# A gated scan and two MLPs on one core: the second layer runs three pairs of blocks behind, its second products are turned, and the first blocks, two buffers and the last stores change

## The chip, the core and the metric

One core of a Trainium2 chip runs the whole kernel. The metric is the device time of one execution in microseconds (us); the profile also has the span from the first to the last instruction. TensorE (PE) multiplies, VectorE (DVE) and ScalarE (ACT) do the elementwise work, SyncE (SP) issues nearly all DMAs. GpSimd (POOL) does nothing here.

## What is computed

```python
# x, f_logit [2, 6080, 256], all float32; 12160 tokens in all
f = lower_bound + (1 - lower_bound) * sigmoid(f_logit)
h[t] = f[t] * h[t-1] + (1 - f[t]) * x[t]            # a scan along each of the 2 sequences
y1 = relu(h @ w_in1) ** 2 @ w_out1                   # layer 1: 256 -> 2048 -> 256
out = elu(y1 @ w_in2) @ w_out2                       # layer 2: 256 -> 2048 -> 256
```

## The kernel before

**Blocks and slots.** The tokens are cut into 24 blocks: one of 384 (`FIRST`), then 23 of 512. A block passes through layer 1 (`m == 0`) and later through layer 2 (`m == 1`). In each layer its 2048 hidden units are taken in 8 groups of 256 (`KG`), and one group of one block in one layer is a *slot*. Two neighbouring blocks form a pair, and their 16 slots are woven into a *run*. The runs of layer 1 and layer 2 alternate, and layer 2 stands `BEHIND = 2` pairs behind: pair 0 and pair 1 in layer 1, then pair 0 in layer 2, pair 2 in layer 1, pair 1 in layer 2 and so on; at the end two runs of layer 2 stand alone.

**A slot.** Float32 accuracy comes from splitting each factor into a high and a low part (fp32r), so each product is three matmuls. The *first product* (from 256 to 256 hidden units, into the PSUM tile `pc`) uses a scheme with 7 instead of 8 block products: 21 matmuls of 256 columns, 9 of them "first" and 12 "later", with a copy of `pc` (`snap`, L654, ACT) between. In the first four blocks of layer 1 (`PLAIN`) it is 12 matmuls of 512 columns instead (L640). Then come the sums on DVE (L657 to L669), the activation (layer 1: relu and square on ACT; layer 2: two ACT passes and one DVE pass, L688), and the split into `g`: `high_part` on ACT (L693) and `low_part` on DVE (L698). The *second product* (`out_mm`, L725, into the PSUM tiles `acc`) reads `g` some two slots later on PE (`LAG`, `AGE`).

**Second products of the two layers.** In layer 1 the weight is the stationary operand and `g` streams past it, 512 columns at a time: 12 matmuls for a slot, and the result stands with the features in the partitions. In layer 2 it is the other way round: 128 tokens of `g` are stationary and 256 columns of `w_out2` stream past, 24 matmuls for a slot of 512 tokens, and the result stands with the tokens in the partitions. So ACT copies it out (L805) and SP stores rows of 256 numbers (L809).

**Scan.** `add_scan` loads half a block of `f_logit` and `x` (L549, four DMAs each, 32 partitions by 8 pieces of 64 numbers), takes tanh on ACT (L553), turns 32x32 squares on DVE (L558), forms gate and feed (L564, L572) and scans (L585), and keeps the carry (L591). `add_parts` makes the sums (L492 to L500) and the split of a block's input (L508 on ACT or as a cast on DVE, L516 on DVE). A block's scans are kept back until the run before its own: half h of the pair's blocks starts at the earliest when the slot `SPREAD` slots ahead begins.

**Weights.** They come in as pieces (`st`, L320 to L328), are rebuilt (L383 to L392) and split (L409 to L415). The second weight stays in SBUF (`wo0`, `wo1`), the first is written back to DRAM (`keep`, `keep_whole`) and streamed from there once for each run (`ws`, L474/L476).

**Order.** All steps are listed with an engine, a cost, a due time and what they read and write (`Order`). `run` then plays a list schedule with these costs: at each point it takes, of the steps that can start within `HOLD` us on an engine, the one with the earliest due time. That fixes the order of each engine's queue; on the chip every queue runs strictly in this order, and an instruction that has to wait holds up everything behind it.

Of the kernel before, what the change touches and what calls it, by code (L numbers as in the profile page):

```python
# [22 lines left out]
BEHIND = 2  # L23
# [23 lines left out]
class Order:  # L47
# [9 lines left out]
    HOLD = 0.2  # L57
# [104 lines left out]
def kernel(  # L162
# [203 lines left out]
    def add_weights(i, m, kind, c, due, wk=None):  # L366
        t = {}

        def load(e):
            t["st"] = new("st", [P, 2, CE // 2, 2], I32)  # L370
            load_w(nc.scalar if i == 0 else nc.sync, t["st"], m, kind, c)
            if i == 0:
                for k in range(KD):
# [24 lines left out]
        def parts():  # L398
            if kind == 0:
                return t["a"], ws_t[m, c][:, 0, 0:4], ws_t[m, c][:, 1, 0:4]  # L400
            v = t["a"].rearrange("p (k e) i -> p k (e i)", k=2)
            return v, *(wo[m][:, 2 * c : 2 * c + 2, x, :] for x in range(2))

        def high_part(e):
            if kind == 0:
# [1 line left out]
            v, hi, _ = parts()
            if e == "ACT":
                nc.scalar.activation(hi, v, AF.Copy)  # L409
            else:  # L410
                nc.vector.tensor_copy(hi, v)
# [8 lines left out]
        def keep_whole(e):  # L420
# [196 lines left out]
    def add_slot(i, m, b, g, wk):  # L617
# [82 lines left out]
        def out_mm(e):  # L700
# [3 lines left out]
            for j in (2 * g + 1, 2 * g):  # L704
# [3 lines left out]
                for q in range(KD if m == 0 else 2 * n // P):  # L708
                    if m == 0:
                        if one:  # L710
                            acc_t[m, b].append(pa.tile([P, TB], F32, tag="acc", name="acc"))
                        a = acc_t[m, b][q][:, : 2 * n]
                        wh, wl = (wo[0][:, j, x, q * P : (q + 1) * P] for x in range(2))
                        three = ((wh, gh), (wh, gl), (wl, gh))
                        clear = one
                    else:
                        if one and q % 2 == 0:
                            acc_t[m, b].append(pa.tile([P, TB], F32, tag="acc", name="acc"))
                        a = acc_t[m, b][q // 2][:, q % 2 * D : (q % 2 + 1) * D]
# [201 lines left out]
```

## Time and profile before

| | |
|---|---|
| median of 3 runs (lowest, highest) | 2083.7 us (2083.47, 2085.03) |
| profiled execution: its time, its span | 2083.75 us, 2082.0 us |
| PE, DVE, ACT busy | 2034.5 us (98%), 1732.3 us (83%), 1697.1 us (82%) |
| chain that ended last, by engine | PE 93%, DVE 4%, ACT 1%, DMA 1% |
| DMA | 268.10 MB, mean 129 GB/s |

A busy PE may still differ in pace: matmuls overlap, so the pace of a group is read from the starts of neighbouring groups, not from the mean duration of one.

### The profile page before, as it was taken

What the parts mean: (1) busy time and instruction counts of PE and PEld (TensorE: products, weight loads), DVE (VectorE), ACT (ScalarE), POOL (GpSimd) and SP (SyncE); (2) the same over time, 40 slices, a digit from 0 to 9 for tenths busy, and PEclk for the clock granted to TensorE, in tenths of its full rate; (3) what the DMA queues carried; (4) which work ended last, traced back from release to release, by engine and by line L of the source; (5) the groups of instructions that cost most, each with busy time, mean ns of one, the idle gap of its engine ahead of it and who ended that gap; (6) DMA issues with size and microseconds to landing.
All of it is one profiled execution on the core that took longest, in us unless ns stands there. A gap on an engine that the chain in (4) does not pass through costs nothing.

```text
span 2082.0 us, 36897 instructions
## 1 busy us (share of the span) xinstructions
PE 2034.5 (98%) x14640; PEld 1925.6 (92%) x14640; DVE 1732.3 (83%) x2830; ACT 1697.1 (82%) x2149; POOL 0.2 (0%) x4
## 2 busy tenths in 40 slices
PE   3999999999999999999999999999999999999998
PEld 3888889999999999999999999999999999999998
DVE  7977996996897798699699689779869968967876
ACT  5887778888888888889788888888888878888886
POOL 0000000000000000000000000000000000000000
PEclk8999999999999999999999999999999999999999
DMA  8787452442343344334244234334433424423321
GB/s 220 229 258 237 143 173 89 128 131 93 124 141 102 119 116 134 116 108 144 89 124 136 92 124 140 105 119 115 135 117 106 140 90 122 133 92 130 104 95 39
DMA packets 207540, 268.10 MB, mean 129 GB/s; under 512 B 110984, under 2 KB 135944, under 8 KB 207368
## 3 DMA queue, kind: packets, MB, share of 16 engines
q1 hardware_dynamic: 206784, 265.21, 40.7%
q8 instruction: 116, 1.90, 0.4%
q10 hardware_dynamic: 584, 0.53, 0.1%
q14 instruction: 56, 0.46, 0.1%
HBM read 221.91 MB, written 43.78 MB: 128 GB/s over the span
## 4 chain that ended last, share of the span: by engine, by line
PE 93%; DVE 4%; ACT 1%; DMA 1%; issue 0%; SPq 0%; DVEq 0%; ACTq 0%
PE acc L725 49%; PE pc L626 40%; PE pc L640 4%; DVE g L698 1%; DVE r L688 1%; DVE r L669 0%; DMA fs<-in_f_logit_dram 0%; DVE F L585 0%; ACT g L693 0%; DMA a<-rd 0%; DVE s L662 0%; ACT s L654 0%; SPq L328 0%; ACT e L682 0%; DVE r L665 0%
## 5 line engine op out<-in xcount | busy, mean ns | idle before, releaser
L725 PE MATMUL acc<-wo,g 128*128 128x256 f32 x4560 | 579.0, 282 | 4.4 <-DVE g L698 2.6
L725 PEld LDWEIGHTS acc<-wo,g 128*128 128x128 f32 x4560 | 560.1, 188 | 5.9 <-DVE g L698 3.9
L725 PE MATMUL acc<-g,wo 128*128 128x512 f32 (+1 forms) x2304 | 552.6, 389 | 0.0
L725 PEld LDWEIGHTS acc<-g,wo 128*128 128x128 f32 x2304 | 420.9, 188 | 78.5 <-DVE g L698 0.3
L626 PE MATMUL pc<-xB,ws 128*128 128x256 f32 x3696 | 486.9, 280 | 4.4 <-ACT s L654 3.6
L626 PE MATMUL pc<-xA,ws 128*128 128x256 f32 (+1 forms) x3696 | 485.8, 280 | 3.2 <-ACT s L654 2.0
L698 DVE TENSOR_TENSOR g<-r,g 128x1024 fp32r<-128x1024 f32 (+1 forms) x384 | 463.8, 1208 | 27.0 <-ACT g L693 24.7
L626 PEld LDWEIGHTS pc<-xB,ws 128*128 128x128 f32 x3696 | 463.6, 188 | 11.6 <-ACT s L654 4.2
L626 PEld LDWEIGHTS pc<-xA,ws 128*128 128x128 f32 x3696 | 463.0, 188 | 10.2 <-ACT s L654 2.4
L693 ACT ACTIVATE g<-r 128x1024 fp32r<-128x1024 f32 (+1 forms) x384 | 402.1, 1047 | 15.6 <-DVE r L688 8.6
L654 ACT ACTIVATE s<-pc 128x768 f32<-128x768 f32 (+1 forms) x352 | 283.5, 805 | 114.3 <-PE pc L626 112.8
L662 DVE TENSOR_TENSOR s<-pc,s 128x256 f32<-128x256 f32 (+1 forms) x352 | 147.8, 420 | 240.0 <-PE pc L626 238.7
L688 DVE SCALAR_TENSOR_TENSOR r<-e,r 128x1024 f32<-128x1024 f32 (+1 forms) x192 | 231.7, 1207 | 24.4 <-ACT e L685 23.7
L669 DVE TENSOR_TENSOR r<-pc,s 128x512 f32<-128x512 f32 (+1 forms) x352 | 241.8, 687 | 9.3
L682 ACT ACTIVATE e<-r 128x1024 f32<-128x1024 f32 (+1 forms) x192 | 202.0, 1052 | 15.0 <-DVE r L665 6.5
L685 ACT ACTIVATE e<-e 128x1024 f32<-128x1024 f32 (+1 forms) x192 | 202.1, 1052 | 6.0
L678 ACT ACTIVATE r<-r 128x1024 f32<-128x1024 f32 (+1 forms) x192 | 202.2, 1053 | 5.6
L675 ACT ACTIVATE r<-r 128x768 f32<-128x768 f32 x160 | 135.5, 847 | 77.7 <-DVE r L665 76.8
L672 ACT ACTIVATE r<-pc 128x256 f32<-128x256 f32 (+1 forms) x352 | 133.4, 379 | 79.5 <-DVE r L669 66.6
L657 DVE TENSOR_TENSOR s<-s 128x256 f32<-128x256 f32 (+1 forms) x352 | 147.1, 418 | 9.8 <-ACT s L654 0.8
L665 DVE TENSOR_TENSOR r<-s 128x256 f32<-128x256 f32 (+1 forms) x352 | 146.7, 417 | 0.0
L585 DVE TENSOR_TENSOR_SCAN F<-fT,carry,xT 128x256 f32<-128x256 f32 (+2 forms) x94 | 65.7, 728 | 0.3
(49 smaller groups left out, 832.1 us busy)
## 6 DMA issues: line engine op xcount, KB each, us to landing
ws<-wd SPq DMA_DIRECT2D x176, 896.0 KB, 5.0
out_dram<-o SPq DMA_DIRECT2D x47, 256.0 KB, 3.8
fs<-in_f_logit_dram SPq DMA_DIRECT2D x184, 64.0 KB, 3.9
xs<-in_x_dram SPq DMA_DIRECT2D x184, 64.0 KB, 2.1
xd<-o SPq DMA_DIRECT2D x46, 256.0 KB, 2.2
F<-xd SPq DMA_DIRECT2D x46, 256.0 KB, 3.3
st<-in_moe_w_out_dram SPq DMA_DIRECT2D x16, 512.0 KB, 4.6
wd<-wp SPq DMA_DIRECT2D x24, 256.0 KB, 4.0
```

The costliest lines, as they stand in the source:

```text
L626: nc.tensor.matmul(t["pc"][:, c], lhsT=ws[:, p, w], rhs=x_t[m, b][:, r, v], start=(which is FIRST_PRODUCTS and q == 0 and c in (1, 2)), st ...
L654: nc.scalar.activation(t["s"], t["pc"][:, 1:4], AF.Copy)
L657: nc.vector.tensor_tensor(t["s"][:, 1], t["s"][:, 1], t["s"][:, 2], op=ALU.add)
L662: nc.vector.tensor_tensor(t["s"][:, 0], t["pc"][:, 0], t["s"][:, 0], op=ALU.add)
L669: nc.vector.tensor_tensor(t["c"][:, 1:3], t["pc"][:, 2:4], u, op=ALU.add)
L678: nc.scalar.activation(t["r"], t["r"], AF.Square)
L682: nc.scalar.activation(t["e"], t["r"], AF.Relu, scale=-1.0)
L685: nc.scalar.activation(t["e"], t["e"], AF.Exp, scale=-1.0)
L688: nc.vector.scalar_tensor_tensor(t["r"], t["e"], 1.0, t["r"], op0=ALU.subtract, op1=ALU.max)
L693: nc.scalar.activation(t["g"][:, 0], t["r"], AF.Copy)
L698: nc.vector.tensor_tensor(t["g"][:, 1], t["r"], t["g"][:, 0].bitcast(F32), op=ALU.subtract)
L725: nc.tensor.matmul(a, lhsT=u, rhs=v, start=clear and k == 0, stop=two and k == 2, skip_group_check=True)
```

## The change

- `FIRST = (512, 384)`: the first block has 512 tokens, the second 384, the other 22 have 512.
- `BEHIND = 3`: pairs 0, 1 and 2 go through layer 1 before pair 0 enters layer 2; three runs of layer 2 stand at the end. `SPREAD = (16, 13, 10, 7)` and `HOLD = 0.1`.
- Two buffers each for `fs` and `xs`, one fewer for `wp` and `a`.
- Layer 2's second product takes the form of layer 1's: the weight is stationary, `g` streams, 12 matmuls of 512 columns for a slot. Its result then has the features in the partitions, so the evacuation moves from ACT copies to DVE: for each half of a block two transposes of 32x32 squares from PSUM into `o`, then four DMAs of 32 partitions with pieces of 64 numbers. The columns of `wo1` are permuted when it is made (two instructions for each half of a piece). The last block's first half is stored from ACT's queue.
- The high parts of the prepared weights and of the plain blocks' inputs are always made on ACT; before, the planner could put them on DVE. In the plan, DMA steps always count as ended by SP, and the first weight's DMA issues are an ACT step; the table load for Exp stands ahead of them.
- The writes of the first weights to DRAM are due 10 and 7 us later.

```diff
-FIRST = (384,)
+FIRST = (512, 384)
-BEHIND = 2
+BEHIND = 3
-SPREAD = (15, 11, 8, 4)
+SPREAD = (16, 13, 10, 7)
-    "fs": 1, "xs": 1, "fT": 1, "xT": 1, "F": 2, "xA": 1, "xB": 1, "ws": 4, "wp": 3, "r": 3, "e": 1,
-    "g": 3, "s": 2, "st": 3, "a": 5, "o": 2, "pc": 2, "acc": 4,
+    "fs": 2, "xs": 2, "fT": 1, "xT": 1, "F": 2, "xA": 1, "xB": 1, "ws": 4, "wp": 2, "r": 3, "e": 1,
+    "g": 3, "s": 2, "st": 3, "a": 4, "o": 2, "pc": 2, "acc": 4,
-    HOLD = 0.2
+    HOLD = 0.1
...
         def load(e):
             t["st"] = new("st", [P, 2, CE // 2, 2], I32)
+            if i == 0:
+                nc.scalar.activation(warm, warm, AF.Exp)
             load_w(nc.scalar if i == 0 else nc.sync, t["st"], m, kind, c)
...
-                nc.scalar.activation(warm, warm, AF.Exp)
...
-            ["DVE", dve(CE, True), high_part, [a], [w], ("ACT", act(CE))],
+            ["ACT", act(CE), high_part, [a], [w]],
...
-            order.add("SP", 0.5, due + 6.0, keep, [w], [("wd", m, c, 0)], None, 512)
-            order.add("SP", 0.5, due + 3.0, keep_whole, [a], [("rd", c)], None, 256)
+            order.add("SP", 0.5, due + 16.0, keep, [w], [("wd", m, c, 0)], None, 512)
+            order.add("SP", 0.5, due + 10.0, keep_whole, [a], [("rd", c)], None, 256)
...
-                        vh, vl = (x[:, q * P : (q + 1) * P] for x in (gh, gl))
-                        wh, wl = (wo[1][:, j, x, :] for x in range(2))
-                        three = ((vh, wh), (vh, wl), (vl, wh))
...
+                    a = acc_t[m, b][q][:, : 2 * n]
+                    wh, wl = (wo[m][:, j, x, q * P : (q + 1) * P] for x in range(2))
+                    for k, (u, v) in enumerate(((wh, gh), (wh, gl), (wl, gh))):
...
-                    nc.scalar.activation(o_t[m, b, q][:, :w], acc_t[m, b][q].rearrange("p (i e) -> p i e", i=2)[:, :w], AF.Copy)
...
+                def turn(c, h=q):
+                    def go(e):
+                        if c == 0:
+                            o_t[m, b, h] = new("o", [P, HB // 32, KD, 32])[:, : n // 64]
+                        v = acc_t[m, b][c][:, h * n // 2 : (h + 1) * n // 2]
+                        nc.vector.transpose(o_t[m, b, h][:, :, c], v.rearrange("p (n i) -> p n i", i=32))
+                    return go
+
+                def store(e, h=q):
+                    t0 = starts[b] + h * n // 2
+                    v = out[t0 : t0 + n // 2, :].rearrange("(n j) (a u) -> a j n u", j=32, a=4)
+                    queue = nc.scalar if e == "ACT" else nc.sync
+                    for a in range(4):
+                        queue.dma_start(v[a], o_t[m, b, h][32 * a : 32 * a + 32].rearrange("j n c i -> j n (c i)"))
+
+                chain(due + 8.0, [
+                    *(["DVE", dve(n // 2), turn(c), [accs[c]], [k]] for c in range(KD)),
+                    ["ACT" if (b, q) == (NBK - 1, 0) else "SP", 1.9, store, [k], (), None, n // 2],
```

What the order of the queues makes of it, at three places.

PE in a run of layer 2, far from the ends. Before:

```order
L626 MATMUL pc<-xB,ws 128x256 x12
L626 MATMUL pc<-xA,ws 128x256 x9
L725 MATMUL acc<-wo_58,g 128x256 x24
L626 MATMUL pc<-xA,ws 128x256 x12
L626 MATMUL pc<-xB,ws 128x256 x9
L725 MATMUL acc<-wo_58,g 128x256 x24
```

The same place after the change (`wo_66` is a second weight):

```order
L634 MATMUL pc<-xB,ws 128x256 x12
L634 MATMUL pc<-xA,ws 128x256 x9
L722 MATMUL acc<-g,wo_66 128x512 x12
L634 MATMUL pc<-xA,ws 128x256 x12
L634 MATMUL pc<-xB,ws 128x256 x9
L722 MATMUL acc<-g,wo_66 128x512 x12
```

The first products stand as before; 24 matmuls of 256 columns became 12 of 512.

DVE in the same kind of run, about its eighth slot. Before (`F<-F` are the sums of `add_parts`, the `fT` and `xT` rows belong to a scan, the other rows to slots):

```order
L492 TENSOR_TENSOR F<-F 128x512
L591 COPY carry<-F 128x2
L496 TENSOR_TENSOR F<-F 128x256
L500 TENSOR_TENSOR F<-F 128x256
L688 SCALAR_TENSOR_TENSOR r<-e,r 128x1024
L662 TENSOR_TENSOR s<-pc,s 128x256
L669 TENSOR_TENSOR r<-pc,s 128x512
L657 TENSOR_TENSOR s<-s 128x256
L665 TENSOR_TENSOR r<-s 128x256
L698 TENSOR_TENSOR g<-r,g 128x1024
L558 STREAM_TRANSPOSE xT<-xs 128x8x2x32
L558 STREAM_TRANSPOSE fT<-fs 128x8x2x32
```

After (L696, L670, L677, L665, L673 and L706 are the six rows of a slot, in the old numbers L688, L662, L669, L657, L665 and L698):

```order
L593 SCALAR_TENSOR_TENSOR F<-fT,carry,xT 128x256
L599 COPY carry<-F 128x2
L566 STREAM_TRANSPOSE xT<-xs 128x8x2x32
L696 SCALAR_TENSOR_TENSOR r<-e,r 128x1024
L670 TENSOR_TENSOR s<-pc,s 128x256
L566 STREAM_TRANSPOSE fT<-fs 128x8x2x32
L677 TENSOR_TENSOR r<-pc,s 128x512
L665 TENSOR_TENSOR s<-s 128x256
L673 TENSOR_TENSOR r<-s 128x256
L706 TENSOR_TENSOR g<-r,g 128x1024
L572 TENSOR_SCALAR fT<-fT,ga,gb 128x256
L670 TENSOR_TENSOR s<-pc,s 128x256
```

The end of one half's scan, and the turns of the next half, now share one slot, and the turn of `fT` and the pass L696 stand among the rows that read `pc`.

SP at the start of the program. Before:

```order
L549 DMA fs<-in_f_logit_dram 32x6x64 x4
L549 DMA xs<-in_x_dram 32x6x64 x4
L328 DMA st<-in_moe_w_in_dram 32x2x512 x8
L549 DMA fs<-in_f_logit_dram 32x6x64 x4
L549 DMA xs<-in_x_dram 32x6x64 x4
L421 DMA rd_140<-a 128x512
```

After:

```order
L557 DMA fs<-in_f_logit_dram 32x8x64 x8
L557 DMA xs<-in_x_dram 32x8x64 x8
L557 DMA fs<-in_f_logit_dram 32x6x64 x4
L557 DMA xs<-in_x_dram 32x6x64 x4
L326 DMA st<-in_moe_w_in_dram 32x2x512 x8
L557 DMA fs<-in_f_logit_dram 32x6x64 x4
```

Both halves of the first block and half of the second now stand ahead of the second and third weight piece.

## Rows read from the trace of the kernel before

**Rows 1.** Page, costliest groups: shapes xcount | busy us, mean ns | idle before.

```profile
L725 PE MATMUL acc<-wo,g 128*128 128x256 f32 x4560 | 579.0, 282 | 4.4 <-DVE g L698 2.6
...
L662 DVE TENSOR_TENSOR s<-pc,s 128x256 f32<-128x256 f32 (+1 forms) x352 | 147.8, 420 | 240.0 <-PE pc L626 238.7
```

**Rows 2.** Waits of PE, whole span: us in total, times, longest us.

```profile
PE pc L640 <- ACT xA L508: 20.5, 1, 20.5
PE pc L640 <- ACT xB L508: 10.1, 1, 10.1
```

**Rows 3.** Windows: a stretch with waits, a layer-2 run, a layer-1 run.

```profile
180.00:320.00 140.00, 131.39 (x954) 122.89 (x953) 128.71 (x234) 107.95 (x148) 0.00 (x0) 1.00 0.52 166
...
708.20:793.70 85.50, 85.50 (x687) 84.03 (x687) 82.78 (x131) 72.15 (x91) 0.00 (x0) 1.00 0.44 130
793.70:877.60 83.90, 83.90 (x567) 77.48 (x565) 59.35 (x99) 69.27 (x91) 0.00 (x0) 1.00 0.32 107
```

**Rows 4.** Timeline, PE, two slots of layer 2, two of layer 1.

```profile
757.16 3.04 PE L725 MATMUL acc<-wo,g 128*128 128x256 f32 x24
760.04 1.58 PE L626 MATMUL pc<-xB,ws 128*128 128x256 f32 x12
...
762.53 3.04 PE L725 MATMUL acc<-wo,g 128*128 128x256 f32 x24
...
836.95 2.91 PE L725 MATMUL acc<-g,wo 128*128 128x512 f32 x12
839.70 1.57 PE L626 MATMUL pc<-xA,ws 128*128 128x256 f32 x12
...
842.16 2.91 PE L725 MATMUL acc<-g,wo 128*128 128x512 f32 x12
```

**Rows 5.** Timeline, DVE, in the same layer-2 run: start us, us.

```profile
753.78 1.23 DVE L698 TENSOR_TENSOR g<-r,g 128x1024 fp32r<-128x1024 f32 x1
754.92 0.68 DVE L492 TENSOR_TENSOR F<-F 128x512 f32<-128x512 f32 x1
...
756.44 1.22 DVE L688 SCALAR_TENSOR_TENSOR r<-e,r 128x1024 f32<-128x1024 f32 x1
...
760.44 0.70 DVE L558 STREAM_TRANSPOSE xT<-xs 128x512 f32<-128x512 f32 x1
...
761.67 1.23 DVE L688 SCALAR_TENSOR_TENSOR r<-e,r 128x1024 f32<-128x1024 f32 x1
...
765.67 0.73 DVE L564 TENSOR_SCALAR fT<-fT,ga,gb 128x256 f32<-128x256 f32 x2
766.44 0.69 DVE L572 SCALAR_TENSOR_TENSOR xT<-fT,xT 128x512 f32<-128x512 f32 x1
767.04 1.22 DVE L688 SCALAR_TENSOR_TENSOR r<-e,r 128x1024 f32<-128x1024 f32 x1
...
771.04 1.39 DVE L585 TENSOR_TENSOR_SCAN F<-fT,carry,xT 128x256 f32<-128x256 f32 x2
772.40 0.42 DVE L662 TENSOR_TENSOR s<-pc,s 128x256 f32<-128x256 f32 x1
```

**Rows 6.** Timeline of the start: SP's queue and ACT.

```profile
6.69 3.99 SPq L328 DMA_DIRECT2D st<-in_moe_w_in_dram  x8
...
8.56 0.51 ACT L553 ACTIVATE fs<-fs 128x384 f32<-128x384 f32 x1
...
10.80 1.80 SPq L549 DMA_DIRECT2D fs<-in_f_logit_dram  x4
...
19.56 0.84 ACT L508 ACTIVATE xA<-F 128x768 fp32r<-128x768 f32 x1 [2.78 <-DVE F L585]
...
38.88 1.06 ACT L508 ACTIVATE xB<-F 128x1024 fp32r<-128x1024 f32 x1 [3.65 <-DVE F L585]
```

**Rows 7.** Timeline of the end: ACT and SP's queue.

```profile
2077.51 1.32 ACT L805 ACTIVATE o<-acc 128x512 f32<-128x512 f32 x2 [3.52 <-PE acc L725]
2078.14 1.09 SPq L809 DMA_DIRECT2D out_dram<-o  x2
```

More of the change, by code (lines that the diff above doesn't have):

```diff
@@ L147, in run @@
             else:
-                ends[n] = (e, t0 + us)
+                ends[n] = ("SP" if s[6] else e, t0 + us)
             for r in ready.values():
@@ L198 @@
     warm = const.tile([P, 1], F32, name="warm")
-    wo = [const.tile([P, KF, 2, D], F32R, name="wo0"), wo1]
+    wo = [const.tile([P, KF, 2, D], F32R, name=f"wo{m}") for m in range(2)]
     pools |= {
@@ L399, in parts @@
             if kind == 0:
-                return t["a"], ws_t[m, c][:, 0, 0:4], ws_t[m, c][:, 1, 0:4]
+                return [(t["a"], ws_t[m, c][:, 0, 0:4], ws_t[m, c][:, 1, 0:4])]
             v = t["a"].rearrange("p (k e) i -> p k (e i)", k=2)
-            return v, *(wo[m][:, 2 * c : 2 * c + 2, x, :] for x in range(2))
+            hi, lo = (wo[m][:, 2 * c : 2 * c + 2, x, :] for x in range(2))
+            if m == 0:
+                return [(v, hi, lo)]
+            return [
+                (v[:, k].rearrange("p (a q j) -> p q a j", a=4, q=KD),
+                 *(u[:, k].rearrange("p (q a j) -> p q a j", a=4, q=KD) for u in (hi, lo)))
+                for k in range(2)
+            ]
         def high_part(e):
@@ L406, in high_part @@
                 ws_t[m, c] = new("ws", [P, 2, NW, P], F32R)
[L407 to L411, printed above, removed]
+            for v, hi, _ in parts():
+                if e == "ACT":
+                    nc.scalar.activation(hi, v, AF.Copy)
+                else:
+                    nc.vector.tensor_copy(hi, v)
         def low_part(e):
-            v, hi, lo = parts()
-            nc.vector.tensor_tensor(lo, v, hi.bitcast(F32), op=ALU.subtract)
+            for v, hi, lo in parts():
+                nc.vector.tensor_tensor(lo, v, hi.bitcast(F32), op=ALU.subtract)
         def keep(e):
@@ L424, in add_weights @@
         steps = [
-            ["SP", 0.1 if i == 0 else 1.9 if m == 0 and kind == 0 else 0.475, load, (), [st], None, 512],
+            ["ACT" if i == 0 else "SP", 5.8 if i == 0 else 1.9 if m == 0 and kind == 0 else 0.475, load, (), [st], None, 512],
             ["ACT", act(CE), scaled, [st], [a]],
@@ L521, in add_parts @@
             chain(due, [
-                ["ACT", act(4 * n), high(0, 4, 0), ready, [X[0]], ("DVE", dve(4 * n, True))],
+                ["ACT", act(4 * n), high(0, 4, 0), ready, [X[0]]],
                 ["DVE", dve(4 * n), low(0, 4, 0), [X[0], *ready], [X[1]]],
@@ L707, in out_mm @@
                 one, two = begin and j % 2 == 1, end and j % 2 == 0
[L708 to L719, printed above, removed]
-                        vh, vl = (x[:, q * P : (q + 1) * P] for x in (gh, gl))
-                        wh, wl = (wo[1][:, j, x, :] for x in range(2))
-                        three = ((vh, wh), (vh, wl), (vl, wh))
-                        clear = one and q % 2 == 0
-                    for k, (u, v) in enumerate(three):
-                        nc.tensor.matmul(a, lhsT=u, rhs=v, start=clear and k == 0, stop=two and k == 2, skip_group_check=True)
-        na = KD if m == 0 else -(-2 * n // HB)
+                for q in range(KD):
+                    if one:
+                        acc_t[m, b].append(pa.tile([P, TB], F32, tag="acc", name="acc"))
+                    a = acc_t[m, b][q][:, : 2 * n]
+                    wh, wl = (wo[m][:, j, x, q * P : (q + 1) * P] for x in range(2))
+                    for k, (u, v) in enumerate(((wh, gh), (wh, gl), (wl, gh))):
+                        nc.tensor.matmul(a, lhsT=u, rhs=v, start=one and k == 0, stop=two and k == 2, skip_group_check=True)
+        na = KD
         if g == 0:
@@ L783, in add_evacuation @@
         due = out_due[m, b, KG - 1] + 12 * ROW * n + 4.0
-        for q, key in enumerate(acc_k[m, b]):
+        accs = acc_k[m, b]
+        for q in range(KD):
+            k = ("o", o_n[0])
+            o_n[0] += 1
             if m == 0:
-                k = ("o", o_n[0] + q)
                 def move(e, q=q):
```

15 lines of the change are left out of this document (1 added, 14 removed).

## The prediction

> **What bounds the kernel now.** I read the waits of PE first. Two hold most of them: 20.5 us until the first matmul and 10.1 us until the second block's input is split [rows 2]. The windows place the rest: between 180 and 320 us PE is busy 131.39 of 140 us, so 8.6 us are idle there, while a run of layer 2 and a run of layer 1 further on are busy to the last tenth [rows 3]. From 320 us on nothing but PE's own pace counts, until the end. So a change pays by making PE's work shorter, or by shortening the start; and whatever other engine it loads must stay under PE in the stretch where the load falls, not on average. There the same windows warn: in the run of layer 2 DVE is busy 82.78 of 85.5 us, in the run of layer 1 only 59.35 of 83.9 [rows 3]. DVE's 83% over the whole span hides a stretch at 97%, because all scans are done in runs of layer 2.
>
> **The turned products.** I take PE's pace from starts. In layer 2 the 24 matmuls take from 757.16 to 760.04, 2.88 us, 120 ns each; in layer 1 the 12 of 512 columns take from 836.95 to 839.70, 2.75 us, 229 ns each [rows 4]. The columns are the same number (6144), so each matmul carries a fixed part, and half as many matmuls save 0.13 us a slot. From one second product to the next the slots take 5.37 and 5.21 us, which says 0.16 [rows 4]; the two runs, 85.5 and 83.9 us for 16 slots of which 12 second products differ, say 0.13 again [rows 3]. There are 4560/24 = 190 such slots [rows 1]: 190 x 0.13 = 25 us, at most 30. The shape after is word for word that of layer 1, so the row prices it directly. I take **-25**.
>
> The Trainium skill has a rule that would make this nearly worthless: TensorE: Matmul & The Clock Gate, section Back-to-back issue gap, gives the isolated gap of a warm matmul as N/2.4 + 2.5 ns, so 109 ns for 256 columns and 216 ns for 512. By it the slot would save 24 x 109.2 - 12 x 215.8 = 31 ns, 6 us in all. The trace disagrees: 120 and 229 ns, a fixed part of some 13 to 16 ns.
>
> **What DVE takes back.** A slot's six DVE instructions take from 756.44 to 760.44, 4.00 us from start to start; the two turns of a scan 1.23 (760.44 to 761.67), two gates 0.77, the feed 0.60, two scans 1.36, the sums with the carry 1.52 [rows 5]. PE's slot will take 5.21. I then count in the order of the queue what stands in slots 3 to 9 of a layer-2 run (from 0). Before: two sets of turns, gates and feeds, one pair of scans, one set of sums, 8.1 us, with seven slots 36.1; PE takes 7 x 5.37 = 37.6 there, and DVE keeps up. After: two sets of turns, two of gates, three feeds, three pairs of scans, two carries and nearly two sets of sums (2.0), 12.1 us, with the slots 40.1 against 7 x 5.21 = 36.5. DVE falls behind by 3.6 us. What it may fall behind is seen in one slot: a `low_part` ends at 755.01 [rows 5], the second product that reads it starts at 757.16 [rows 4], 2.15 us later; two shorter second products in between leave some 1.85. So PE waits about 1.75 us in each such run. In the new order a pass that waits for nothing of PE's often stands between L670 and L677, where before the second waited for the first to end, and that gives some tenths back: 1.5. Eight runs of layer 2 have this order (the first one, which makes weights too, and the last three, which have no scans, are counted apart): 8 x 1.5 = **+12**. Bounds: 0 if DVE's small overlaps give 1.75 us more; 3.5 us a run, 28, if the pass that now stands before L677 (1.14 us) keeps `pc` from PE so much longer, which leaves 0.7 of the 1.85, and a part of the 2.7 us in which DVE stood idle in the run before [rows 3] stays.
>
> The transposes that evacuate layer 2 are not in this sum. A 256-wide DVE instruction that reads PSUM takes 420 ns [rows 1], 0.35 from start to start, so a pair of blocks costs 8 x 0.35 = 2.8 us; twice that if a transpose from PSUM were half as fast. But by the order they stand at the end of the run (four) and one slot into the next run (four), where DVE has 1.2 us a slot over for ten slots. ACT loses the two copies of a block, about 0.6 us each as in the tail [rows 7], and needs nothing of it.
>
> **The start.** Before, the second half of the first block stood on SP behind eight weight DMAs: issued at 10.80 [rows 6]. After, both halves are issued at once, but then DVE has the first block's two halves back to back: from the end of the first tanh (before it began at 8.56 [rows 6]; the table load and six DMA issues still stand ahead of it, in another order: I take an end at 8.2) two halves at 1.23 + 0.77 + 0.60 + 1.36 + 0.12 = 4.1 us, one weight piece (three passes of 0.65, estimated from the turns of the same width) and about 0.9 of stalls, in all 19.2. So the first matmul starts where it did, at 20.5, with 128 more tokens behind it. Then two halves of 192 columns (3.3 each, 4.1 cut by a quarter), the first block's low part (1.2) and two and a half weight pieces bring DVE to 32; ACT has one slot's three passes (1.06 each, as the split at 38.88 [rows 6]) and two weight passes in front and splits the second block at about 34.5, where before it began at 38.88 [rows 6]. Its low part follows a microsecond later, at 35.5 instead of 41.3: 5.8 us. PE has by then done 36 matmuls of 512 columns instead of 384, 36 x (0.229 - 0.174) = 2.0 us more of its work. Together **-8**; bounds 0 (ACT, which now also makes every weight's high part, holds the split back to 41) and -12 (the 10.1 us of [rows 2] go and the wider block counts as well).
>
> **180 to 320 us.** These 8.6 us [rows 3] come from DVE making layer 2's weights and the sums of layer 1's beside the scans of the first alternating runs. With three pairs ahead the same passes spread over another 83 us run. The first run of layer 2 still has two pairs of slots whose DVE order holds 12 to 13.5 us, by the prices above, against 9 to 10 of PE; counted in the same way some 4.6 us remain: **-4**, between -8.6 and 0.
>
> **The end.** Before, ACT copies the last two tiles in 1.32 us and SP issues two DMAs [rows 7]; the span ends 2.8 us after the second issue (2079.2). After, four transposes (1.4 us) and four issues of about 0.45 (1.80 for four, [rows 6]) stand behind the last matmul; the other half's issues go beside them on ACT. **+1.5**, between 0.5 and 4. The pieces of 256 bytes are what the loads of `x` have now, and layer 2's stores have 20 us until their buffers are wanted again.
>
> **Sum**, against the profiled execution's 2083.75 us (span 2082.0), which is the median to 0.05: 2083.75 - 25 + 12 - 8 - 4 + 1.5 = 2060.
>
> **Rivals.** (B) DVE fits: the order has the scans denser, but where a slot's passes no longer wait for each other it gains a quarter of a microsecond a slot. The +12 goes: **2048**. For it: before, DVE was at 97% without one wait of PE. (C) DVE, or the later release of `pc`, costs 3.5 us a run, +28: **2076**. The runs of both layers would then take 2 x 83.4 + 3.5 = 170.3 us against 169.4 (85.5 + 83.9) before, and only the ends gain. (D) The fixed part does not fall with the number of matmuls but goes with the columns, so that 512 columns take 240 ns in layer 2: nothing is saved, 2060 + 25 = **2085**. Against it: the 229 ns of layer 1 in the same form. The Trainium skill's rule above would leave 6 of the 25. (E) The other side. `o` has two buffers, so the second block's transposes wait on DVE until the first block's stores have landed, eight DMA issues on a queue that also waits for PE to free a weight buffer; a DVE that stands there holds up `snap`'s readers and all slots. The place is the first slots of every layer-1 run. The forecast without the +12 gains 35.5 us, 3.0 for each of 12 such runs; DVE has 2 to 3.8 us of lead there. Should a store land so late that DVE stands over about 6 us a run, the kernel is slower than before; at 7 us, **2096** with nothing from C. Against it: two slots, 10 us, lie between the two blocks' transposes, and eight issues take 3.6.
>
> **How the numbers follow.** Forecast (A) 0.47, B 0.26, C 0.18, D 0.05, E 0.04. A alone reaches from 2052 to 2068. From 2043 (B with a start of -12) to 2079 (C with 3 us less at the start) lies all of A, most of B and most of C, about 0.8. A measurement tells a difference of about 0.2%, 4.2 us, so faster is under 2079.5: A, B and nearly all of C, 0.90; same 0.06 (D and a little of C); slower 0.04.
>
> **What would show it.** Second products at 2.75 us and slots at 5.21 in the three runs of layer 2 at the end: the 25 is right. PE waits at the second product (L722) or the first (L634) about the ninth slot of the middle runs of layer 2, and none in runs of layer 1: the 12 is right, and its size is read off the periods of two runs, 169 us or so. No such waits: B. Waits for `pc` rather than `g`: C's mechanism. The second block's split at 34 to 36 us, and under 5 us of PE's waits before 50 us, show the start. DVE idle before its transposes until a store's DMA would show E. I am wrong most easily in the 12: it is a difference of two sums of 40 us, and 0.1 us in a slot's passes moves it by 5.

## The result, and the profile after

The changed kernel takes 2066.1 us (median of 4 runs, 2066.0 to 2066.8), the kernel before 2084.3 us (4 runs). The ratio is 0.9914, with a 95% interval of 0.9896 to 0.9931: 18 us faster, six slower than the 2060 forecast. The profiled execution took 2066.0 us, with a span of 2064.2.

The page after, busy times and the group of the second products ([rows 1] before), then PE's waits ([rows 2]):

```profile
PE 2017.2 (98%) x12384; PEld 1802.5 (87%) x12384; DVE 1727.0 (84%) x2902; ACT 1688.4 (82%) x2141; POOL 0.2 (0%) x4
...
L722 PE MATMUL acc<-g,wo 128*128 128x512 f32 x4608 | 1114.7, 390 | 8.1 <-DVE g L706 6.8
```

```profile
PE pc L648 <- ACT xA L516: 21.4, 1, 21.4
PE acc L722 <- DVE g L706: 6.8, 15, 1.2
PE pc L634 <- ACT s L662: 5.5, 7, 1.2
PE pc L634 <- ACT r L655: 2.9, 1, 2.9
```

The second block's wait (10.1 us in [rows 2]) is gone. One long wait for an ACT pass is new (L655, 2.9 us), and the waits of second products for `g` grew from 5 to 15 (2.6 us in all before). The rest shows in the stages. I take a run as the time from its first product to the next run's, read off PE's timeline:

| stretch | before, us | after, us | difference |
|---|---|---|---|
| until the first matmul | 20.5 | 21.4 | +0.9 |
| first run | 89.1 | 79.9 | -9.3 |
| second run (plain blocks too) | 88.6 | 91.4 | +2.8 |
| first other run of layer 1 | 87.0 | 87.7 | +0.7 |
| first run of layer 2 | 84.3 | 84.9 | +0.6 |
| nine more runs of layer 1 | 83.92 each | 83.41 each, the first 83.98 | -4.0 |
| eight more runs of layer 2, with scans after the change | 85.43 each | 84.7 to 85.3 | -3.6 |
| two runs of layer 2, without scans after the change | 85.43 each | 83.41 each | -4.0 |
| last run to the end of the span | 102.8 | 101.0 | -1.8 |

The second products of a run's last three slots fall into the next run, so a run of layer 1 also gains a little (83.92 to 83.41).

The windows of six of these runs after the change ([rows 3] before; columns: length, then busy time and instructions of PE, PEld, DVE, ACT and POOL, granted clock, DMA share, GB/s):

```profile
101.20:192.60 91.40, 87.72 (x385) 71.25 (x383) 80.58 (x157) 66.22 (x88) 0.00 (x0) 1.00 0.75 228
192.60:280.30 87.70, 86.22 (x528) 76.48 (x529) 75.47 (x144) 79.04 (x117) 0.00 (x0) 0.98 0.68 218
280.30:365.30 85.00, 81.05 (x531) 73.84 (x531) 79.04 (x140) 67.37 (x92) 0.00 (x0) 1.00 0.44 131
785.90:870.80 84.90, 84.59 (x530) 75.44 (x529) 82.43 (x137) 72.29 (x91) 0.00 (x0) 1.00 0.43 130
870.80:954.30 83.50, 83.50 (x531) 75.62 (x530) 59.77 (x103) 67.92 (x86) 0.00 (x0) 1.00 0.33 108
1879.80:1963.20 83.40, 83.40 (x531) 75.52 (x530) 73.52 (x115) 70.75 (x85) 0.00 (x0) 1.00 0.34 108
```

The last row is layer 2 with nothing in its way: 83.4 us, 2.0 under the 85.43 of before. The fourth is the same work beside the scans, with DVE busy for 82.43 of 84.9: 1.5 us of the 2.0 are lost again. Where, PE's timeline shows, from the tenth slot of that run:

```profile
833.89 2.91 PE L722 MATMUL acc<-g,wo 128*128 128x512 f32 x12
836.64 1.57 PE L634 MATMUL pc<-xB,ws 128*128 128x256 f32 x12
838.17 1.32 PE L634 MATMUL pc<-xA,ws 128*128 128x256 f32 x9
839.34 3.04 PE L722 MATMUL acc<-g,wo 128*128 128x512 f32 x12
...
844.88 2.96 PE L722 MATMUL acc<-g,wo 128*128 128x512 f32 x12
...
850.80 2.81 PE L722 MATMUL acc<-g,wo 128*128 128x512 f32 x11 [0.26 <-DVE g L706]
```

A second product undisturbed takes 2.75 us (833.89 to 836.64, 229 ns a matmul, as layer 1's in [rows 4]), and an undisturbed slot 5.21. Between the second products here lie 5.45 and 5.54 us. Only one of the delays is listed as a wait, 0.26 us. The row of a matmul lasts 390 ns in the mean and the next one starts after 229, so a delay of a tenth or two of a microsecond looks like busy time. The busy share of PE hides it, and the starts show it.

### The profile page after: what moved, and what is told of

Same layout as the page of the kernel before. It is cut to its first block, busy times and chain, and to the rows that moved or that the text cites. A ratio compares the mean times of both kernels' runs of the same rounds, so it can differ in the third digit from the quotient of the medians.

```text
span 2064.2 us, 32500 instructions
## 1 busy us (share of the span) xinstructions
PE 2017.2 (98%) x12384; PEld 1802.5 (87%) x12384; DVE 1727.0 (84%) x2902; ACT 1688.4 (82%) x2141; POOL 0.2 (0%) x4
## 4 chain that ended last, share of the span: by engine, by line
PE 57%; DVE 31%; ACT 6%; DMA 2%; issue 2%; SPq 1%; DVEq 0%; ACTq 0%
PE acc L722 30%; PE pc L634 26%; DVE g L706 7%; DVE r L696 5%; DVE r L677 4%; DVE F L593 2%; DVE s L665 2%; DVE r L673 2%; DVE s L670 2%; PE pc L648 2%; DVE fT L572 1%; DVE fT L566 1%; ACT g L701 1%; ACT e L693 1%; DVE xT L580 1%
## 5 line engine op out<-in xcount | busy, mean ns | idle before, releaser
L722 PE MATMUL acc<-g,wo 128*128 128x512 f32 x4608 | 1114.7, 390 | 8.1 <-DVE g L706 6.8
L722 PEld LDWEIGHTS acc<-g,wo 128*128 128x128 f32 x4608 | 839.1, 188 | 172.7 <-DVE g L706 16.0
L634 PE MATMUL pc<-xA,ws 128*128 128x256 f32 x3696 | 487.6, 281 | 7.7 <-ACT s L662 4.2
L634 PEld LDWEIGHTS pc<-xA,ws 128*128 128x128 f32 x3696 | 467.8, 188 | 26.9 <-ACT s L662 9.3
L634 PE MATMUL pc<-xB,ws 128*128 128x256 f32 (+1 forms) x3696 | 483.2, 280 | 1.3 <-ACT s L662 1.3
L706 DVE TENSOR_TENSOR g<-r,g 128x1024 fp32r<-128x1024 f32 (+1 forms) x384 | 463.2, 1206 | 16.1 <-ACT g L701 13.9
L670 DVE TENSOR_TENSOR s<-pc,s 128x256 f32<-128x256 f32 (+1 forms) x352 | 146.6, 416 | 229.9 <-PE pc L634 229.7
L662 ACT ACTIVATE s<-pc 128x768 f32<-128x768 f32 (+1 forms) x352 | 282.4, 802 | 45.7 <-PE pc L634 45.1
L696 DVE SCALAR_TENSOR_TENSOR r<-e,r 128x1024 f32<-128x1024 f32 x192 | 231.2, 1204 | 26.3 <-ACT e L693 25.6
L677 DVE TENSOR_TENSOR r<-pc,s 128x512 f32<-128x512 f32 (+1 forms) x352 | 240.5, 683 | 7.3 <-ACT r L680 2.5
L690 ACT ACTIVATE e<-r 128x1024 f32<-128x1024 f32 x192 | 201.8, 1051 | 28.3 <-DVE r L673 22.8
L686 ACT ACTIVATE r<-r 128x1024 f32<-128x1024 f32 x192 | 202.1, 1053 | 4.7
L693 ACT ACTIVATE e<-e 128x1024 f32<-128x1024 f32 x192 | 201.6, 1050 | 5.1
L665 DVE TENSOR_TENSOR s<-s 128x256 f32<-128x256 f32 (+1 forms) x352 | 147.1, 418 | 9.9 <-ACT s L662 3.4
L673 DVE TENSOR_TENSOR r<-s 128x256 f32<-128x256 f32 (+1 forms) x352 | 147.0, 418 | 0.0
L648 PE MATMUL pc<-xA,ws 128*128 128x512 f32 x192 | 50.8, 415 | 22.9 <-ACT xA L516 21.4
L648 PEld LDWEIGHTS pc<-xA,ws 128*128 128x128 f32 x192 | 37.6, 198 | 33.0 <-ACT xA L516 21.4
```

The costliest lines, as they stand in the source:

```text
L634: nc.tensor.matmul(t["pc"][:, c], lhsT=ws[:, p, w], rhs=x_t[m, b][:, r, v], start=(which is FIRST_PRODUCTS and q == 0 and c in (1, 2)), st ...
L662: nc.scalar.activation(t["s"], t["pc"][:, 1:4], AF.Copy)
L665: nc.vector.tensor_tensor(t["s"][:, 1], t["s"][:, 1], t["s"][:, 2], op=ALU.add)
L673: nc.vector.tensor_tensor(t["c"][:, 3], t["s"][:, 0], t["s"][:, 1], op=ALU.add)
L677: nc.vector.tensor_tensor(t["c"][:, 1:3], t["pc"][:, 2:4], u, op=ALU.add)
L686: nc.scalar.activation(t["r"], t["r"], AF.Square)
```

## The experiments

All were timed in 3 rounds beside the kernel before (median 2084.0 to 2084.2 us in each group of runs). Line numbers are each kernel's own.

**1. The scans by the old numbers.**

```diff
-SPREAD = (16, 13, 10, 7)
+SPREAD = (15, 11, 8, 4)
```

> The changed kernel (2066.1 us) with the scans started by the numbers of before, SPREAD (15, 11, 8, 4), and nothing else. Theory 1, DVE's order: by the prices of the trace DVE's passes in a middle run of layer 2 fall behind PE's slots of 5.21 us by up to 3.7 us (tenth slot) in the changed order, and by up to 2.1 us (last slot) in this one, against a cover of some 1.85 us. So the eight runs of layer 2 with scans go from 84.9 back to about 83.6 us: 8 x 1.3 = 10 us less, some 2056, and no run of layer 1 gets longer. Rival, the passes between the two that read pc: they stand there in this order too, so the runs stay at 84.9 and the time at 2066 (within 1.5 us).

Measured: 2067.6 us (2066.7 to 2067.8), not the 2056 of theory 1. The runs of layer 2 fell to 84.1, but those of layer 1 rose from 83.4 to 84.5: the scans end later and meet the evacuation's transposes at the boundary. This order alone only moves the backlog.

**2. High parts free to go on DVE.**

```diff
-            ["ACT", act(CE), high_part, [a], [w]],
+            ["DVE", dve(CE, True), high_part, [a], [w], ("ACT", act(CE))],
...
-                ["ACT", act(4 * n), high(0, 4, 0), ready, [X[0]]],
+                ["ACT", act(4 * n), high(0, 4, 0), ready, [X[0]], ("DVE", dve(4 * n, True))],
```

> The changed kernel (2066.1 us) with the high parts of the weights and of the plain inputs free to go on DVE again. The stretch from 100 to 370 us took 3.5 us longer than expected at the least: the second run takes 91.4 us for 88.6 before. Theory 1, ACT's fixed high parts: PE waits 2.93 us at 189.3 for a pass of ACT that stood behind a weight's high part, which itself waited 4.5 us for DVE; freed, the second run falls to about 88.6 and the time to 2062 to 2064. Rival, DVE has too many passes there in either case (weights, scans of three pairs and the sums in the first 280 us): eight more casts go to DVE, the second run stays at 91 or grows, and the time is 2066 or more.

Measured: 2070.4 us (2069.8 to 2070.9). The second run became 95.4 us:

```profile
102.80:198.20 95.40, 90.47 (x385) 73.63 (x386) 82.08 (x158) 71.32 (x95) 0.00 (x0) 0.96 0.77 241
```

So theory 1 falls: putting these passes on ACT alone spares time. How much of the 4.0 us between 91.4 and 95.4 is DVE's is open, since the granted clock was also lower here (0.96 for 1.00).

**3. Layer 2's second products as before.** The other edits of the change stay.

```diff
-                for q in range(KD):
+                for q in range(KD if m == 0 else 2 * n // P):
...
+                        vh, vl = (x[:, q * P : (q + 1) * P] for x in (gh, gl))
+                        wh, wl = (wo[1][:, j, x, :] for x in range(2))
```

> The changed kernel (2066.1 us) with layer 2's second products, its evacuation and the order of the columns of its second weight as they were before; scans, blocks and the third pair stay as changed. Theory 1: the turn is worth 24 us of PE (190 slots x 0.125), and DVE's late order costs 1.5 us in each of eight runs only because PE's slots became shorter; with slots of 5.34 us again that loss shrinks to 0 to 0.5 us, and the end gives back 2: 2066 + 24 - 10 - 2 = 2078, between 2075 and 2081. Rival, the 1.5 us a run are not DVE's: then they stay, and it is 2088.

Measured: 2074.2 us (2073.9 to 2074.7), just under the range of theory 1; its rival said 2088. A run of layer 2 with scans (first row), the layer-1 run behind it, and a run without scans (last):

```profile
786.30:871.50 85.20, 85.20 (x686) 83.63 (x685) 82.68 (x137) 72.52 (x91) 0.00 (x0) 1.00 0.43 130
871.50:955.30 83.80, 83.80 (x566) 77.41 (x565) 57.59 (x95) 68.76 (x89) 0.00 (x0) 1.00 0.31 108
1886.10:1971.60 85.50, 85.50 (x723) 85.50 (x722) 72.33 (x107) 71.15 (x88) 0.00 (x0) 1.00 0.30 106
```

With the same scans, DVE costs nothing here: 85.2 with them, 85.5 without. So the 1.5 us a run exist because PE's slots became shorter. The turn leaves 8.2 us of its 24: besides DVE's 12 and the end's 2, the first two runs after the third pair have nothing of it (85.0 and 83.7 here, 84.9 and 84.0 with it).

**4. The turn alone, on the kernel before.**

```diff
-                for q in range(KD if m == 0 else 2 * n // P):
+                for q in range(KD):
...
-                    nc.scalar.activation(o_t[m, b, q][:, :w], acc_t[m, b][q].rearrange("p (i e) -> p i e", i=2)[:, :w], AF.Copy)
+                        nc.vector.transpose(o_t[m, b, h][:, :, c], v.rearrange("p (n i) -> p n i", i=32))
```

> The kernel before (2084.3 us) with the turned second products and their evacuation alone; blocks, pairs, buffers and scans as before. Theory 1: 24 us less of PE, 2 us more at the end, and DVE, whose order of before falls behind by 2 us at most, costs 0 to 0.8 us in each of nine runs: 2062 to 2069. The rest of the change (start, third pair, spread of the scans) would then be worth 4 us or less together, though the start alone gained 9: the spread and the third pair gave it back. Rival, DVE cannot take the evacuation beside its 97% in runs of layer 2 whatever the order: 2.5 us or more in each run, 2080 or more.

Measured: 2079.3 us (10 runs, 2077.2 to 2081.3), ten above the top of the expectation, at the edge of the rival. The first two runs that alternate, and two in the middle:

```profile
197.30:284.50 87.20, 80.16 (x518) 74.29 (x517) 80.95 (x156) 63.75 (x92) 0.00 (x0) 0.96 0.46 145
284.50:372.60 88.10, 84.58 (x531) 75.84 (x530) 67.67 (x119) 68.10 (x88) 0.00 (x0) 1.00 0.41 131
709.60:793.80 84.20, 84.20 (x530) 75.62 (x529) 82.12 (x131) 71.91 (x90) 0.00 (x0) 1.00 0.44 130
793.80:878.20 84.40, 83.97 (x531) 75.75 (x530) 62.39 (x109) 66.61 (x86) 0.00 (x0) 1.00 0.33 108
```

A pair of runs takes 168.6 us, as with the new order (168.4) and with experiment 1 (168.7), where PE at the pace of the changed kernel would need 166.8. I took this for one loss, DVE's work, in three orders. The starts show that here it is another. PE in the middle of the run of layer 2, then at the boundary of the two runs:

```profile
731.61 2.97 PE L723 MATMUL acc<-g,wo 128*128 128x512 f32 x12
734.42 1.57 PE L635 MATMUL pc<-xA,ws 128*128 128x256 f32 x12
...
736.88 2.97 PE L723 MATMUL acc<-g,wo 128*128 128x512 f32 x12
...
810.25 1.31 PE L635 MATMUL pc<-xB,ws 128*128 128x256 f32 x9 [0.43 <-DVE r L678]
```

No second product here starts late or stops in the middle; each is slower throughout, 2.81 us instead of 2.75, its matmuls evenly 230 to 238 ns apart, and the slot takes 5.27 instead of 5.21. For 16 slots that is 0.9 of the 1.8 us. Nearly all of the rest is one stall at the boundary, where `pc` is freed late by DVE (L678 is L677 of the changed kernel): rival C's mechanism. That the three sums agree is chance. The first pair of runs loses 4 us against before (84.3 and 87.0), the end 3.

**5. The gates on ACT.** If DVE's work is the cause, less of it must help wherever it stands.

```diff
-                nc.vector.tensor_scalar(f[:, c], f[:, c], ga[:, c : c + 1], gb[:, c : c + 1], op0=ALU.mult, op1=ALU.add)
+                nc.scalar.activation(f[:, c], f[:, c], AF.Identity, bias=gb[:, c : c + 1], scale=ga[:, c : c + 1])
...
-            *(["DVE", dve(n, True), gate(c), [("bound",)], [fT]] for c in range(KD)),
+            *(["ACT", act(n), gate(c), [("bound",)], [fT]] for c in range(KD)),
```

> The changed kernel (2066.1 us) with the two gate passes of each half scan made by ACT instead of DVE. The last four runs left this theory 2, DVE's budget: whatever the order, DVE has by the prices of the trace 85.6 us of work in a run of layer 2 with scans, and PE's work is now 83.4; before it was 85.4. This takes 2.1 us out of that run (and some out of the first four), so the eight runs of 84.9 fall to about 83.6: 2054 to 2057. Rival, the passes between the two that read pc hold PE (an order matter): the runs stay at 84.9, and the scan's way over ACT adds waits: 2066 or more.

Measured: 2058.3 us (2057.3 to 2059.2), 8 less. The second run, and a middle run of layer 2:

```profile
101.00:188.40 87.40, 86.84 (x386) 71.45 (x384) 75.04 (x142) 70.73 (x98) 0.00 (x0) 1.00 0.78 235
...
781.30:865.70 84.40, 84.12 (x530) 75.51 (x530) 80.23 (x129) 75.19 (x99) 0.00 (x0) 1.00 0.44 131
```

The second run gives back 4.0 us (the one behind it nothing, 87.8 for 87.7), each middle run of layer 2 0.6, less than half of what was expected there.

**6. Both.** Experiment 5 with `SPREAD = (15, 11, 8, 4)`.

> The same with SPREAD (15, 11, 8, 4). With these numbers and the gates on DVE the runs of layer 2 took 84.1 us and those of layer 1 84.5, 168.6 for a pair of runs. Theory 2: DVE's work in a run of layer 2 is 82.3 us now, 1.1 under PE's 83.4, and nowhere more than half a microsecond behind: both runs at 83.4 to 83.6, a pair at 167.1, and 2054 to 2058. Rival: the transposes of the evacuation at the start of layer 1's runs hold PE whatever else DVE has to do: layer 1's runs stay at 84.5, 2064 or more.

Measured: 2054.2 us (2053.6 to 2054.6), ratio 0.9856 (0.9841 to 0.9871): the fastest of all. A middle pair takes 167.4 us:

```profile
779.70:863.40 83.70, 83.70 (x530) 75.44 (x529) 79.92 (x129) 73.25 (x96) 0.00 (x0) 1.00 0.46 133
863.40:947.10 83.70, 83.70 (x531) 75.57 (x530) 60.98 (x105) 68.35 (x87) 0.00 (x0) 1.00 0.33 107
```

The spread that gained nothing by itself now gains 4 us. The transposes at the boundary are no fixed loss. The 0.3 us a run over 83.4 stand at second products, rows of PE and of DVE:

```profile
853.71 3.08 PE L722 MATMUL acc<-g,wo 128*128 128x512 f32 x12
856.62 2.63 PE L634 MATMUL pc<-xB,ws 128*128 128x256 f32 x21
859.09 3.10 PE L722 MATMUL acc<-g,wo 128*128 128x512 f32 x12
...
852.72 1.22 DVE L706 TENSOR_TENSOR g<-r,g 128x1024 fp32r<-128x1024 f32 x1
```

The second product takes 2.91 us instead of 2.75, and the first product behind it its undisturbed 2.47. DVE's `low_part`, which the second product reads, ends at 853.94, after that product has begun. So these 0.3 us are DVE's, not the release of `pc`.

**7. One DVE pass of the scan twice.**

```diff
+        def turn2(e):
+            nc.vector.transpose(t["xT"].rearrange("p c (n i) -> p n c i", i=32), t["xs"])
...
+            *([["DVE", dve(N), turn2, [xs], [xT]]] if after else []),
```

> The changed kernel (2066.1 us) with the turn of x done twice by DVE in each half scan of the 18 blocks that are scanned in runs of layer 2: 4 x 0.63 = 2.5 us more of DVE in each of nine such runs. Theory 2, DVE's budget: nothing is left, so each run grows by 2.5 us, 9 x 2.5 = 22: 2086 to 2090. Rival, the 1.5 us a run are lost to the place of single passes and DVE still has the idle time that its windows show (2.5 us of 84.9): half of it or less is seen, 2066 to 2077.

Measured: 2074.2 us (2074.0 to 2074.9), 8 more where 22 were expected, in the range of the rival.

```profile
789.20:875.00 85.80, 85.25 (x530) 75.48 (x529) 84.17 (x141) 71.97 (x90) 0.00 (x0) 1.00 0.44 129
```

So DVE is no strict budget. Of 2.5 us more, 0.85 lengthen the run; DVE's idle time in it falls from 2.5 (84.9 - 82.43) to 1.6; the rest is carried into the run of layer 1, whose second `low_part` ends 2.0 us ahead of its product instead of 2.7. A pass costs PE a third of its length here.

**8. Two pairs between the layers.**

```diff
-BEHIND = 3
+BEHIND = 2
```

> The changed kernel (2066.1 us) with two pairs of blocks between the layers as before. The prediction's view, the third pair spreads the making of weights and saves 4 us: 2070. Theory 3, the third pair puts its scans and its slots (three passes of DVE each) beside the weights in the second and third run and costs time there: by the prices DVE has 67 us of work in the second run for 79, 90 in the third for 76, 62 in the fourth for 78, so 88.6 + 86 + 84.5 + the rest as it is, 4 us less: 2062.

Measured: 2062.25 us (2061.0 to 2062.7), as theory 3 has it: the third pair costs 3.8 us in the changed kernel. But theory 3 came to its sum by 88.6, 86 and 84.5 us for the second to fourth run, and these measured otherwise, so the closeness of the total is in part luck:

```profile
99.70:186.40 86.70, 86.70 (x386) 71.65 (x385) 70.29 (x133) 72.57 (x98) 0.00 (x0) 1.00 0.78 257
186.40:274.40 88.00, 81.81 (x529) 73.82 (x528) 83.38 (x161) 69.91 (x105) 0.00 (x0) 1.00 0.61 188
274.40:361.40 87.00, 83.84 (x531) 76.64 (x530) 64.31 (x115) 67.56 (x89) 0.00 (x0) 0.98 0.40 124
```

**9 and 10. All three edits, and the same with a more even spread.** To experiment 6 comes the first of these edits, and then the second:

```diff
-BEHIND = 3
+BEHIND = 2
...
-SPREAD = (15, 11, 8, 4)
+SPREAD = (16, 12, 9, 5)
```

> The changed kernel with three edits: gates on ACT, SPREAD (15, 11, 8, 4) (these two: 2054.2 us) and two pairs between the layers instead of three (alone: 3.9 us less than the changed kernel). If the gains stand for different work they add: 2050. If both mend the same lack, DVE's time beside the weights in the second to fourth run, little is left to gain there: with runs of 86.5, 87, 86 us where the gates alone gave 87.3, 87.6, 84.1, 85.2 before the pattern sets in, 2053 to 2054.

> The same with SPREAD (16, 12, 9, 5). By the prices of the trace no slot of a pair of runs leaves DVE more than 1.6 us behind, 1.7 with (15, 11, 8, 4), and the sum over the slots falls from 12.3 to 10.8; but the run of layer 2 then has 83.8 us of DVE for 82.3. If the backlog at a slot decides: a pair of runs at 167.1 to 167.4 us, the same as or up to 2 us under the other. If the sum over a run decides: 1.5 us more in each of nine runs at most, half of it seen as when work was doubled, 5 us over the other.

Measured: 2057.1 us (2056.0 to 2058.0) and 2058.6 (2057.5 to 2059.1). Neither adds. With the gates on ACT the third pair is worth 3 us instead of costing 4: the first run of layer 2, with weights and scans at once, takes 90.0 us with two pairs. A middle pair of runs takes 167.4 with the one spread, 167.7 with the other, so neither the greatest backlog nor the sum by itself forecast it.

**11. The start as before.**

```diff
-FIRST = (512, 384)
+FIRST = (384,)
-    "fs": 2, "xs": 2, "fT": 1, "xT": 1, "F": 2, "xA": 1, "xB": 1, "ws": 4, "wp": 2, "r": 3, "e": 1,
+    "fs": 1, "xs": 1, "fT": 1, "xT": 1, "F": 2, "xA": 1, "xB": 1, "ws": 4, "wp": 2, "r": 3, "e": 1,
```

> The changed kernel (2066.1 us) with the start as before: first block 384 (the 23 others 512), one buffer each for f_logit and x. The first run took 79.9 us for 89.1 before, the second 91.4 for 88.6. Theory: the start is worth its 9 us, but part of the second run's 2.8 us more is the same DVE work come later; undone, the first run is 88 to 89, the second 88.6 to 90: 2071 to 2075. Rival, the wait for the second block only moves and what the start gains is lost again in the second run whatever else is there: 2066 to 2068.

Measured: 2069.9 us (2068.4 to 2071.2), between the two. The second and third run:

```profile
110.10:198.70 88.60, 88.60 (x385) 72.15 (x384) 76.55 (x148) 73.46 (x99) 0.00 (x0) 1.00 0.81 247
198.70:283.70 85.00, 82.94 (x518) 74.64 (x517) 67.17 (x126) 69.72 (x101) 0.00 (x0) 0.98 0.55 176
```

The new start is 8.9 us ahead when the second run begins (101.2 for 110.1), 3.3 at the start of the fourth (280.35 for 283.66), 3.8 in the end.

**12. Last stores on SP alone.**

```diff
-                    ["ACT" if (b, q) == (NBK - 1, 0) else "SP", 1.9, store, [k], (), None, n // 2],
+                    ["SP", 1.9, store, [k], (), None, n // 2],
```

> The changed kernel (2066.1 us) with all last stores on SP. The last matmul is followed by 5.9 us, before by 3.8. Theory: four issues of 0.45 us more stand ahead of the last one on SP, and some of them are done before the last transposes end: 1 us more, 2067.1. Rival, the way of the last DMA's data sets the end and the issues are hidden: 2066 to 2066.4.

Measured: 2066.9 us (2065.4 to 2067.2). The medians don't separate the two; in the profile 6.8 us lie between the last matmul and the end, for 5.9 with two queues, as the theory has it.

## Why the forecast was right in kind and six microseconds short

**The turn, -25: right for the turn, but PE gained 30.** A run of layer 2 without scans takes 85.44 us in experiment 3 and 83.41 in the changed kernel. These 2.03 us for 16 slots are 0.127 a slot, 24 for 190, where the prediction said 0.13. By the rule of the Trainium skill that it weighed (TensorE: Matmul & The Clock Gate, Back-to-back issue gap) 16 slots would gain an estimated half microsecond; the trace has four times that.

Against the kernel before, PE gained more than the turn. A run of each layer together took 85.43 + 83.92 us and takes 2 x 83.41 where DVE does not delay it: 2.5 us for 16 slots of layer 2, 0.16 a slot, 30 for 190. The prediction saw the 0.16 in the slots and set it at its bound, because it divided the difference of the two runs by 12 second products; as each run carries three of the run before it, 10 is right. The 6 us beyond the turn's 24 came with other edits: without the turn a slot of layer 2 takes 5.34 us in experiment 3 for 5.37 before, and with the turn alone 5.27 in experiment 4 for 5.21. No run separates them. One that the list of changes does not name is the place of layer 2's second weight in SBUF:

```diff
-    late = ctx.enter_context(tc.tile_pool(name="late", bufs=1))
-    wo1 = late.tile([P, KF, 2, D], F32R, name="wo1")
...
-    wo = [const.tile([P, KF, 2, D], F32R, name="wo0"), wo1]
+    wo = [const.tile([P, KF, 2, D], F32R, name=f"wo{m}") for m in range(2)]
```

**DVE, +12: right in place and size.** 84.9 less 83.4 is 1.5 in each of eight runs, 12.5 in all, in the tenth to fifteenth slot, and none in runs of layer 1 but 0.6 in the first of them. Experiment 3 shows that it comes from PE's shorter slots, experiments 5 to 7 that DVE's work makes it. My reason for 1.5, a backlog of 3.6 us less a cover of 1.85, fits this order, but is no law: two sets of gates fewer in the seven slots leave 0.2 us by the same sum, and 0.9 us a run stayed in experiment 5. Rival C's mechanism, a late release of `pc`, has a share: of the 1.5 us some 0.4 stand at first products (836.64 to 839.34 is 2.70 us for 2.46 undisturbed), the rest at second products. Rival D fell with second products of 2.75 us. For E there is no sign: DVE's transposes waited 3.0 us in all, and only for PE.

**The start, -8: right where it was counted, and then lost.** Rows of ACT, DVE and PE ([rows 6] before):

```profile
33.84 0.83 ACT L516 ACTIVATE xB<-F 128x768 fp32r<-128x768 f32 x1
...
35.13 0.95 DVE L524 TENSOR_TENSOR xB<-F,xB 128x768 fp32r<-128x768 f32 x1
...
36.13 2.18 PE L648 MATMUL pc<-xB,ws 128*128 128x384 f32 x11 [0.97 <-DVE xB L524]
```

The split begins at 33.84 (forecast 34.5), PE goes on behind the low part at 36.13 (35.5; before 41.29), and the second run starts 8.4 us earlier. Counted were the 5.2 us of this and 2.0 for the wider block. Not counted were 2.3 us of a lower clock that went away (last section); the rest of the run lost 1.1 again, so the closeness of 8.4 to 8 is partly luck. By experiment 11 3.8 us last.

**180 to 320 us, -4: this term is wrong.** The step was that with three pairs ahead "the same passes spread over another 83 us run". The second run and the two behind it became longer instead, by 2.8, 0.7 and 0.6 us, though PE's shorter slots should have taken about 2 us from the last. I had counted DVE's passes in the first run of layer 2, not in the second run, which the new start brings 8.4 us earlier, with weights, scans and slots still to be made by the same DVE. What PE met there, rows of ACT, then of DVE:

```profile
189.20 0.72 ACT L417 ACTIVATE wo<-a 128x256 fp32r<-128x256 f32 x2 [4.54 <-DVE a L391]
...
191.59 1.00 ACT L655 ACTIVATE r<-pc 128x1024 f32<-128x1024 f32 x1
...
186.23 0.69 DVE L500 TENSOR_TENSOR F<-F 128x512 f32<-128x512 f32 x1
...
188.48 0.69 DVE L391 SCALAR_TENSOR_TENSOR a<-st,a 128x512 int32<-128x512 int32 x1
```

ACT stands 4.5 us at a weight's high part, because DVE comes to that weight only after a scan and its sums; the pass behind it that PE waits for (L655, 2.9 us) is late with it. Blaming ACT's fixed queue was my first theory, and experiment 2 refuted it; taking passes from DVE cured the second run (91.4 to 87.4, the wait 2.9 to 0.6), though not the one behind it. Experiment 11 shows that the third pair alone does not do it: with the late start the same two runs take 88.6 and 85.0. The new start and the third pair together put more on DVE there than it can do in time; either one undone, or DVE relieved, and the loss shrinks.

**The end, +1.5: 2.1 by the trace.** Four transposes and four issues stand behind the last matmul ([rows 7] before), 5.9 us in all for 3.8:

```profile
2057.61 1.47 DVE L805 STREAM_TRANSPOSE o<-acc 128x256 f32<-128x256 f32 x4 [2.21 <-PE acc L722]
2058.79 1.97 ACTq L813 DMA_DIRECT2D out_dram<-o  x4
```

In spans the kernel gained 17.8 us. PE's pace gave 30 (forecast 25), DVE took 12.5 (12), the start gave 8.4 (8) and the end took 2.1 (1.5). That makes 23.8, so by the balance the stretch from the second run on cost about 6 where 4 were forecast as gain. Ten microseconds of error there stand against 5 at PE that the forecast did not count; that the total is only six off is luck. Left open is which edit gave the 6 us beyond the turn. (The lower end of the stated range, 2043, is 2044 by its own terms, 2048 less 4.)

## What to carry to other kernels

When the bounding engine gets faster, do not stop at its own gain: count the next engine's work against the new, shorter time, slot by slot. Here DVE at 97% took back 12 of 30 us that it had nothing to do with, and moving two small passes to an engine with room was worth more than the other order of the same passes. Count every stretch that a gain moves as well: work that arrives earlier must be made earlier, and two edits that look good at the start can spoil each other. And read the pace of the bounding engine in every kernel of a series before naming a cause: 0.06 us in each slot gave the same sum as a late DVE.

## What the runs showed of the hardware

Before the change PE ran slowly behind its second wait. Windows of the kernel before, then of the one after:

```profile
44.00:46.00 2.00, 2.00 (x6) 1.61 (x5) 2.00 (x4) 0.00 (x0) 0.00 (x0) 0.50 0.42 130
46.00:48.00 2.00, 2.00 (x12) 1.92 (x12) 1.83 (x4) 1.64 (x2) 0.00 (x0) 0.97 0.70 187
```

```profile
44.00:46.00 2.00, 2.00 (x11) 1.65 (x9) 1.93 (x3) 2.00 (x4) 0.00 (x0) 1.00 0.77 242
```

After 10.1 us without a matmul the granted clock is 0.50, the lower level of 1.2 GHz, until 46 us, and a matmul of 512 columns starts every 427 ns; after the change the wait is 1.0 us, the clock stays at 1.00 and the pace at 230 to 238. Before, eleven matmuls from 41.29 to 46.13 us of PE's timeline took 4.84 us where 11 x 0.229 = 2.5 would do: a wait of 10 us had a tail of 2.3 that no list of waits shows. The Trainium skill (TensorE: Matmul & The Clock Gate, Wait — 56ns, not 53.3ns?) gives starts N/1.2 ns apart at the lower clock, 426.7 for 512 columns, and the trace agrees to the nanosecond; at the full clock its 215.7 is 13 ns short of the 229 here.

A shorter wait can have such a tail and need not. Behind the 2.9 us that PE waits at the end of the second run, the changed kernel (first row) and experiment 1 with the same wait (second row) differ:

```profile
192.60:194.60 2.00, 1.96 (x9) 1.96 (x10) 2.00 (x5) 1.97 (x3) 0.00 (x0) 0.50 1.00 388
191.60:193.60 2.00, 2.00 (x13) 1.87 (x14) 2.00 (x5) 1.97 (x3) 0.00 (x0) 1.00 1.01 367
```

The run behind took 87.7 and 87.6 us all the same. So in these runs the length of a wait alone did not tell whether the clock fell, and here, where PE waits for other engines as well, the lower clock cost nothing that the length of the run shows.
